# A port term in a kernel's planner, two-source work kept off GpSimd in the second half, and sums of x formed when an attention pair ends

## The chip, the core and the metric

The kernel runs on one core of a Trainium2 chip. The core has a matrix engine (TensorE, PE in the profile; PEld is its weight load, which overlaps it), three engines that work on whole tiles (VectorE or DVE, ScalarE or ACT, GpSimd or POOL) and SyncE (SP), which issues nearly all of this kernel's DMAs. The metric is the device time of one execution in microseconds. TensorE is granted one of two clocks, 1.2 or 2.4 GHz; the profile gives the granted clock of a stretch as a share of the upper one.

## What is computed

Causal attention over 4 batches of 12 heads, 448 positions and 64 columns a head; its result, laid out as 1792 rows of 768, goes through a two-layer network with a squared ReLU. Everything is float32. The reference, cut to this:

```python
scores = np.matmul(q, k.transpose(0, 1, 3, 2)) / np.sqrt(64)
scores = np.where(np.triu(np.ones((448, 448), bool), k=1), -1e9, scores)
attn = np.exp(scores - scores.max(-1, keepdims=True))
attn = attn / (attn.sum(-1, keepdims=True) + 1e-09)
x = np.matmul(attn, v).transpose(0, 2, 1, 3).reshape(1792, 768)
h = np.maximum(x @ w_in, 0.0)          # w_in 768 x 2048
return h * h @ w_out                   # w_out 2048 x 768
```

w_in and w_out arrive as 64-bit floats and are decoded on the chip.

## The kernel before

**Splits.** For the network every float32 operand is held as two fp32r tiles: a rounded copy ("hi") and the rest ("lo", the whole less hi). A product takes three matmuls: hi·hi, hi·lo, lo·hi. `split` (L297) makes both: hi by a copy on POOL or ACT, lo by a subtraction with two sources on DVE or POOL. Names: `x` (attention's result, the matmuls' moving operand), `wi` and `wo` (pieces of w_in and w_out), `g` (the squared ReLU), all with a hi and a lo; `words` is a scratch area for pieces of the weights, for x read back and for sums; `r0`..`r5` are 128x448 work tiles; `ps` is a bank of PSUM; `acc` holds the output.

**Stages.** The rows are taken in two halves (batches 0 and 1, then 2 and 3), the 2048 hidden columns in four groups. A group is an H stage (x times w_in, ReLU, square, split into g) and an O stage (g times w_out, added into acc: 14 pieces of 4 products, 168 matmuls). First the attention of head pairs 0 to 11 runs; then, during the four groups of the first half, the attention of pairs 12 to 23 is put between the matmuls. Its results wait in DRAM (`x_dram`, 12 tiles of 128x448). In the first half an H stage has 8 units of 18 matmuls (`h_unit`, L553). In the second half `h_pair` (L681) multiplies 2x2 blocks with 7 products instead of 8, by Winograd's scheme: 2 x 7 x 9 = 126 matmuls. It needs seven parts of x for each of three columns, "11", "21", "22" and the sums t1 to t4 (`x_parts`, L589: 4 loads, 4 sums, 7 splits a column, so 12 sums and 21 splits in all), and seven parts of w_in for each pair of hidden tiles (`w_parts`, L622). w_in and w_out are decoded in the first half (`piece`, L497), split, and kept in DRAM as hi and lo (`wi_split`, `wo_split`), from which the second half reads them; `w_parts` adds hi and lo again (`whole`, L632), forms sums (`made`, L667) and splits them (`done`, L662).

**What sets the order.** `Plan.emit` (L97) is a list scheduler that runs once, when the kernel is built. Each operation has a rank, dependences, tiles to take and give back, and one or more "ways": an engine and a duration from a formula (`t_dve`, `t_pool` and others, L147 to L160). It takes the ready operation that can start first, chooses the way that ends first, and so fixes the order on each engine. On the chip each engine runs its list in that order, held up by semaphores. One line gives a start: `max(free[e], at)`, the later of the engine's free time and the operands'. `attended` and `entered` (L848 on) are points in the plan behind which tiles of the attention stage and of `h_unit` may be taken for the parts of x. What stands in a tile kind at one time is bounded by caps: `r=2, xs=2, y=6` and `fz=5, s=3, xp=4`.

Of the kernel before, what the change touches and what calls it, by code (L numbers as in the profile page):

```python
# [36 lines left out]
class Plan:  # L37
# [59 lines left out]
    def emit(self):  # L97
        free = [1.0, 1.9, 3.4, 2.7, 0.7, 0.7]
        ready = [o for o in self.ops if o.left == 0]
        order = []  # L100
        while ready:
            best = None
            for o in ready:
                at = o.ready + (self.ISSUE if o.ways[0][0] >= DMA else 0.0)
                if o.take:
# [7 lines left out]
                    (max(free[e], at) + us + self.BIAS[e], max(free[e], at), i, e)  # L113
                    for i, (e, us, _) in enumerate(o.ways)
# [6 lines left out]
            free[e] = end = start + o.ways[i][1]  # L121
            order.append((start, len(order), o, i))
# [41 lines left out]
def kernel(  # L164
# [17 lines left out]
    nc = tc.nc  # L182
# [73 lines left out]
    plan.pool("r", tiles("r", NR, [P, S], F32), r=2, xs=2, y=6)  # L256
    plan.pool("f", [], fz=5, s=3, xp=4)
# [50 lines left out]
    def attention(s, n, at):  # L308
# [70 lines left out]
        def normalise(c, keys, at):  # L379
            def operands():  # L380
                return probabilities(c), probabilities(c), s.sm[:, c:c + 1]
            plan.op(at, [
                (POOL, 0.0005 * CW[c] + 0.34, lambda: nc.gpsimd.tensor_scalar(  # L383
                    *operands(), 1.0, op0=ALU.mult, op1=ALU.mult)),
                (DVE, t_dve(CW[c], True) + 0.5, lambda: nc.vector.tensor_scalar(
                    *operands(), None, op0=ALU.mult)),
# [57 lines left out]
        plan.op(at, [(DVE, 0.45, inverse)], [], keys)  # L444
# [15 lines left out]
        else:  # L460
            xs = Hold("r", "xs")
            plan.op(at, [
                on_act(S, lambda: xs.t, lambda: av.t[:, :S], True),
                (DVE, t_dve(S) + 0.05, lambda: nc.vector.tensor_copy(xs.t, av.t[:, :S])),
            ], [av], [xs], take=xs, drop=[av])
            plan.op(at, [(DMA, 0.7, lambda: nc.sync.dma_start(out=x_dram[n - NA], in_=xs.t))],
                    [xs], [("xd", n - NA)], drop=[xs])
# [4 lines left out]
    wo_dram = nc.dram_tensor("wo_split", (NG, 2 * GF, P, 2, CH), F32, kind="Internal").ap()  # L472

    def wo_part(a, ch):
        return late["wo"][:, :, a, ch * CH:(ch + 1) * CH].bitcast(F32)

    def keep(rank, kind, gr, a, ch, after):
        if kind == "i":
            def go():
                for i in range(2):  # L480
                    nc.sync.dma_start(
                        out=wi_dram[gr, :, a // CB, :, i, a % CB].rearrange("f p n -> p f n"),
                        in_=wi_t[:, i, a].bitcast(F32).rearrange("p (f n) -> p f n", n=P))
            plan.op(rank, [(DMA, 1.9, go)], [(("wi", a), 0), (("wi", a), 1)], [("wid", gr, a)], after)
            return
        plan.op(rank, [(DMA, 1.7, lambda: nc.sync.dma_start(
            out=wo_dram[gr, a + GF * ch], in_=wo_part(a, ch)))],
            [(("wo", a, ch), 0), (("wo", a, ch), 1)], [("wod", gr, a, ch)])

    def fetch(rank, gr, a, ch):  # L490
        plan.op(rank, [(DMA, 1.7, lambda: nc.sync.dma_start(
            out=wo_part(a, ch), in_=wo_dram[gr, a + GF * ch]))],
            [("wod", gr, a, ch)], [(("wo", a, ch), 0), (("wo", a, ch), 1)])
# [3 lines left out]
    def piece(rank, kind, gr, a, ch, after):  # L497
# [23 lines left out]
        def dst(i):  # L521
# [11 lines left out]
            z(), z(), 3, None, op0=ALU.logical_shift_left))], [], [zt])  # L533
        plan.op(rank - 2, [on_dve(n, z, z, b, ALU.add, 0.3)], [bt], [zt], drop=[bt])
        plan.op(rank - 2, [(DVE, t_dve(n) + 0.2, lambda: nc.vector.scalar_tensor_tensor(
            out=z(), in0=word(1), scalar=-2 ** 31, in1=z(),
            op0=ALU.bitwise_and, op1=ALU.bitwise_or))], [raw], [zt], drop=[raw])
        split(rank, n, lambda: dst(0), lambda: dst(1), zf, [zt], key, after, [zt])
        pieces.extend(plan.ops[mark:])
# [4 lines left out]
    def squared(f, h, r, rank):  # L544
        def rt():
            return r.t
        plan.op(rank, [on_dve(S, rt, rt, rt, ALU.mult, 0.4), on_pool(S, rt, rt, rt, ALU.mult),
                       on_act(S, rt, rt, func=AF.Square)], [], [r])
# [32 lines left out]
    x7, owned = {}, {}  # L581

    def combine(rank, n, dst, a, b, op, reads, writes, **kw):
        def of(h):
            return lambda: h.t[:, :n]
        plan.op(rank, [on_dve(n, of(dst), of(a), of(b), op), on_pool(n, of(dst), of(a), of(b), op)],
                reads, writes, **kw)

    def x_parts(i, rank, after):  # L589

        B = {}
        for m, (key, n) in enumerate((("11", i), ("12", NP + i), ("22", NP + CB + i), ("21", CB + i))):
# [300 lines left out]
```

## Time and profile before

| | us |
|---|---|
| time, median of 3 runs (lowest, highest) | 632.28 (631.47, 632.42) |
| the profiled execution | 631.39 |
| its span, first to last instruction | 629.6 |
| PE busy / DVE busy / ACT busy / POOL busy | 604.6 / 367.3 / 325.2 / 371.8 |
| mean granted clock of TensorE | 0.989 |

The span is what the trace covers; the profiled execution is 1.8 us longer than its span and 0.9 us shorter than the median. By the trace the attention alone lasts to about 75 us, the first half to about 401 us, the second to the end. Matmuls are pipelined: the trace shows each as 0.34 to 0.39 us long while they start about 0.2 us apart, so an unbroken stage is read from the distance of starts. A row of the waits view names who was waited for; a releaser is inferred, and where the engine named had work of its own held up, the wait began further back.

### The profile page before, as it was taken

To read this page: it belongs to the slowest core of one execution; us is meant where nothing else is said; L and a number is where in the kernel's file an instruction comes from. 1 tells how busy PE (TensorE), PEld (TensorE's weight loads), DVE (VectorE), ACT (ScalarE), POOL (GpSimd) and SP (SyncE) were. 2 spreads that over 40 slices of the span, in tenths; PEclk is the share of its full clock that TensorE was granted. 3 is DMA by queue.
4 is the path that set the end of the run, shared out by engine and by line. 5 is a ranking of instruction groups with operands and counts; after the bars stand their busy time and mean duration, and the time that the engine had idled before them with its cause. 6 is when DMAs were issued, how large, how long until landed. Compare 5 with 4: busy or idle time off the path is not lost.

```text
span 629.6 us, 11242 instructions
## 1 busy us (share of the span) xinstructions
PE 604.6 (96%) x3864; PEld 532.2 (85%) x3864; DVE 367.3 (58%) x822; ACT 325.2 (52%) x803; POOL 371.8 (59%) x454
## 2 busy tenths in 40 slices
PE   4989999999999899999999999799999999999997
PEld 2656677898888798898898889799999999999997
DVE  5679976386767788767874219944015424533222
ACT  4679896865687646587556433345235003302400
POOL 2456766644767763787846459989238706914510
PEclk9799999999999899999999999999999999999999
DMA  9877852797897899886964144873234234333022
GB/s 146 164 187 132 180 122 56 170 324 260 217 258 227 230 256 275 228 251 177 257 199 156 50 129 154 280 223 101 100 110 141 82 126 145 101 101 102 1 89 87
DMA packets 175225, 103.77 MB, mean 165 GB/s; under 512 B 115264, under 2 KB 164928, under 8 KB 175168
## 3 DMA queue, kind: packets, MB, share of 16 engines
q1 hardware_dynamic: 171456, 102.59, 58.9%
q10 hardware_dynamic: 3712, 0.46, 0.5%
q8 instruction: 30, 0.49, 0.3%
q14 instruction: 27, 0.22, 0.1%
HBM read 69.60 MB, written 33.42 MB: 164 GB/s over the span
## 4 chain that ended last, share of the span: by engine, by line
PE 60%; DVE 4%; issue 1%; DMA 1%; POOL 0%; ACT 0%; DVEq 0%; ACTq 0%
PE ps L754 9%; PE ps L756 9%; PE ps L755 9%; PE ps L693 5%; PE ps L695 5%; PE ps L697 5%; PE ps L559 3%; PE ps L561 3%; PE ps L560 3%; PE ps L417 2%; PE ps L397 2%; PE ps L357 2%; DVE x L287 1%; DVE acc L287 1%; DVE words L287 1%
## 5 line engine op out<-in xcount | busy, mean ns | idle before, releaser
L756 PE MATMUL ps<-wo,g 128*128 128x384 f32 x448 | 150.4, 336 | 2.5 <-POOL g L291 2.5
L754 PE MATMUL ps<-wo,g 128*128 128x384 f32 x448 | 152.4, 340 | 0.0
L755 PE MATMUL ps<-wo,g 128*128 128x384 f32 x448 | 150.3, 336 | 0.0
L383 POOL TENSOR_SCALAR ap<-ap,asm 128x64 f32<-128x64 f32 (+6 forms) x120 | 73.9, 636 | 43.6 <-DVE asm L442 22.2
L287 DVE TENSOR_TENSOR acc<-ps,acc 128x384 f32<-128x384 f32 x84 | 46.1, 553 | 84.1 <-PE ps L756 70.5
L284 ACT ACTIVATE r<-ps 128x448 f32<-128x448 f32 x60 | 32.8, 546 | 107.5 <-PE ps L697 79.3
L756 PEld LDWEIGHTS ps<-wo,g 128*128 128x128 f32 x448 | 84.4, 188 | 2.8 <-POOL g L291 2.8
L754 PEld LDWEIGHTS ps<-wo,g 128*128 128x128 f32 x448 | 84.5, 189 | 1.3 <-issue 0.8
L370 DVE CUSTOM_DVE_ANT_0 ps<-ps,mask 128x448 f32<-128x448 f32 (+6 forms) x168 | 68.7, 443 | 27.5 <-PE ps L357 18.3
L755 PEld LDWEIGHTS ps<-wo,g 128*128 128x128 f32 x448 | 84.6, 189 | 0.2
L284 ACT ACTIVATE words<-words 128x384 f32<-128x384 f32 (+3 forms) x112 | 64.5, 614 | 25.7 <-DMA words<-in_moe_w_in_dram 8.6
L559 PE MATMUL ps<-x,wi 128*128 128x448 f32 x192 | 74.4, 387 | 0.3 <-DVE x L287 0.3
L561 PE MATMUL ps<-x,wi 128*128 128x448 f32 x192 | 70.3, 366 | 0.9 <-POOL wi L291 0.9
L560 PE MATMUL ps<-x,wi 128*128 128x448 f32 x192 | 70.2, 365 | 0.0
L374 ACT ACTIVATE ap<-ps,mx 128x448 f32<-128x448 f32 (+6 forms) x126 | 58.7, 483 | 21.3 <-DVE mx L370 15.6
L287 DVE TENSOR_TENSOR r<-ps,r 128x448 f32<-128x448 f32 x40 | 24.9, 623 | 73.7 <-PE ps L697 71.1
L294 POOL TENSOR_SCALAR wi<-words 128x512 fp32r<-128x512 f32 (+1 forms) x27 | 15.9, 589 | 85.1 <-PE ps L695 57.2
L291 POOL TENSOR_TENSOR g<-r,g 128x448 fp32r<-128x448 f32 x50 | 59.5, 1195 | 5.5 <-ACT g L284 2.7
L284 ACT ACTIVATE r<-r 128x448 f32<-128x448 f32 x76 | 43.9, 577 | 21.8 <-DVE r L287 20.4
L693 PE MATMUL ps<-x,wi 128*128 128x448 f32 x138 | 51.3, 372 | 3.7 <-ACT r L284 3.7
L291 POOL TENSOR_TENSOR wi<-words,wi 128x512 fp32r<-128x512 f32 (+1 forms) x41 | 52.3, 1279 | 1.7
L695 PE MATMUL ps<-x,wi 128*128 128x448 f32 x138 | 51.2, 371 | 0.0
(94 smaller groups left out, 1157.4 us busy)
## 6 DMA issues: line engine op xcount, KB each, us to landing
words<-in_moe_w_in_dram SPq DMA_DIRECT2D x24, 512.0 KB, 4.8
words<-in_moe_w_out_dram SPq DMA_DIRECT2D x32, 384.0 KB, 4.1
wi_split<-wi SPq DMA_DIRECT2D x48, 256.0 KB, 3.6
wo_split<-wo SPq DMA_DIRECT2D x32, 384.0 KB, 3.9
wo<-wo_split SPq DMA_DIRECT2D x32, 384.0 KB, 5.1
wi<-wi_split SPq DMA_DIRECT2D x18, 384.0 KB, 3.5
out_dram<-acc SPq DMA_DIRECT2D x28, 192.0 KB, 1.9
v<-in_v_dram SPq DMA_DIRECT2D x24, 192.0 KB, 4.6
```

Of the source, the lines that this page charges most:

```text
L284: return (ACT, t_act(n, psum, more), lambda: nc.scalar.activation(dst(), src(), func, **kw))
L287: return (DVE, t_dve(n) + more, lambda: nc.vector.tensor_tensor(out=dst(), in0=a(), in1=b(), op=op))
L291: lambda: nc.gpsimd.tensor_tensor(out=dst(), in0=a(), in1=b(), op=op))
L383: (POOL, 0.0005 * CW[c] + 0.34, lambda: nc.gpsimd.tensor_scalar(*operands(), 1.0, op0=ALU.mult, op1=ALU.mult)),
L559: nc.tensor.matmul(o, w[:, 0], x[:, 0], start=c == 0, stop=False)
L560: nc.tensor.matmul(o, w[:, 0], x[:, 1], start=False, stop=False)
L561: nc.tensor.matmul(o, w[:, 1], x[:, 0], start=False, stop=c == NP - 1)
L693: nc.tensor.matmul(o, w.t[:, 0, c], x[:, 0], start=begin and c == 0, stop=False, skip_group_check=True)
L695: nc.tensor.matmul(o, w.t[:, 0, c], x[:, 1], start=False, stop=False, skip_group_check=True)
L754: nc.tensor.matmul(res(), g[:, 0], w[:, 0], start=f == 0, stop=False)
L755: nc.tensor.matmul(res(), g[:, 0], w[:, 1], start=False, stop=False)
L756: nc.tensor.matmul(res(), g[:, 1], w[:, 0], start=False, stop=f == GF - 1)
```

## The change

**Planner.** `emit` keeps one more time, `port`: a way marked `SHARED` starts no earlier than the last such way has ended, on whichever engine. Marked are two-source operations on DVE and POOL, and DVE's fast one-source ones; POOL's copies (L294) and its normalise operation of attention (L383) aren't. Several durations change. `two_sources` offers DVE and POOL both until `pool_too[0]` is set to False, which is done before the parts of x and the second half are planned: from there such work goes on DVE alone.

**Sums of x.** When an attention pair of the first half's stages ends, `spill` stores its result as before and, for the pairs of the last batch, also forms t1 (columns 0 to 2) or t1 to t4 from PSUM and from what it reads back, in `r` tiles, and stores those in `xt_dram`. `x_parts` is replaced by `x_part`: one load and one split for each of 21 parts, in the order of the seven products. Caps change: xs 4, xp 3, fo 2.

**Weights.** w_out is kept whole (`wo_whole`, one store of half the size), read back and split again in the second half; w_in is kept whole too for groups 1 to 3 (`wi_whole`) and split only for groups 0 and 3. So `whole` runs in group 0 alone, and parts "11", "12" and "22" of groups 1 and 2 get a split that they didn't need before. The second half runs its groups from 3 to 0, and group 3's w_out stays in SBUF. The matmuls are the same in kind and number.

```diff
@@ emit
-        order = []
+        order, port = [], 0.0
...
                 w = min(
-                    (max(free[e], at) + us + self.BIAS[e], max(free[e], at), i, e)
-                    for i, (e, us, _) in enumerate(o.ways)
+                    (max(free[w[0]], at, port if len(w) > 3 else 0.0) + w[1] + self.BIAS[w[0]],
+                     max(free[w[0]], at, port if len(w) > 3 else 0.0), i, w[0])
+                    for i, w in enumerate(o.ways)
                 )
...
             free[e] = end = start + o.ways[i][1]
+            if len(o.ways[i]) > 3:
+                port = max(port, end)
...
 def t_dve(n, fast=False):
-    return n / 1920 + 0.25 if fast else n / 960 + 0.15
+    return n / 1920 + 0.15 if fast else n / 960 + 0.15
 def t_pool(n, two=False):
-    return n * 0.0027 + 0.04 if two else n / 1200 + 0.26
+    return n * 0.0021 + 0.21 if two else n / 1200 + 0.22
...
+    def two_sources(*args):
+        return [on_dve(*args, 0.03) + SHARED] + ([on_pool(*args)] if pool_too[0] else [])
...
-        plan.op(rank, [on_dve(n, lo, src, lambda: hi().bitcast(F32), ALU.subtract, 0.4),
-                       on_pool(n, lo, src, lambda: hi().bitcast(F32), ALU.subtract)],
+        plan.op(rank, two_sources(n, lo, src, lambda: hi().bitcast(F32), ALU.subtract),
                 list(reads) + [(key, 0)], [(key, 1)], after, drop=drop)
...
-                (POOL, 0.0005 * CW[c] + 0.34, lambda: nc.gpsimd.tensor_scalar(
+                (POOL, 0.00083 * CW[c] + 0.3, lambda: nc.gpsimd.tensor_scalar(
...
+        if second and c < CB:
+            h = loaded(x_dram[c], ("xd", c))
+            less(h, [av])
+            stored(h, *t_place(1))
+        elif second:
+            t1 = loaded(*t_place(1))
+            x21 = loaded(x_dram[c], ("xd", c))
+            x12 = loaded(x_dram[n - CB], ("xd", n - CB))
+            less(t1, [av])
+            plan.op(at, two_sources(S, lambda: x21.t, lambda: x21.t, lambda: t1.t, ALU.subtract),
+                    [t1], [x21])
+            less(x12, [av])
+            stored(t1, *t_place(2))
+            stored(x12, *t_place(3))
+            stored(x21, *t_place(4))
...
+    def x_part(key, i, rank, after):
+        t, h = x7[key, i], Hold("f", "xp")
...
+        plan.op(rank - 4, [(DMA, 0.9, lambda: nc.sync.dma_start(out=h.t, in_=place))], [saved], [h], take=h)
+        split(rank, S, lambda: t()[:, 0], lambda: t()[:, 1], lambda: h.t, [h], ("x7", key, i), [after], [h])
...
-    keys = [(key, i) for key in ("11", "t2", "21", "t3", "t1", "t4", "22") for i in range(CB)]
+    keys = [(OTHER[key], i) for key in SEVEN for i in range(CB)]
+    pool_too[0] = False
...
-        for gr in range(NG):
+        for gr in range(NG - 1, -1, -1):
             begin, rank = group(ph, gr, rank, 1.0, begin)
```

Two places show what this does to the order. In the rows a line number, the operation, the tiles out<-in and the shape stand; the numbers at the names tell tiles apart.

DVE in the last O stage of the first half, before: `words<-words,r` and `r<-words,r` are sums of x or of w_in, `x2_` and `x` a lo of a part of x.

```order
L287 TENSOR_TENSOR r5_102<-words_96,r4_101 128x448
L287 TENSOR_TENSOR acc_1379<-ps6_119,acc_1379 128x384
L287 TENSOR_TENSOR x2_81<-r4_101,x2_81 128x448
L287 TENSOR_TENSOR acc_1379<-ps2_115,acc_1379 128x384
L287 TENSOR_TENSOR x0_79<-words_96,x0_79 128x448
L287 TENSOR_TENSOR x1_80<-words_96,x1_80 128x448
L287 TENSOR_TENSOR words_96<-words_96,r5_102 128x448
L287 TENSOR_TENSOR acc_1379<-ps3_116,acc_1379 128x384
```

The same place on DVE after the change:

```order
L293 TENSOR_TENSOR acc_1368<-ps4_117,acc_1368 128x384
L293 TENSOR_TENSOR acc_1368<-ps6_119,acc_1368 128x384
L293 TENSOR_TENSOR x2_3_3908<-words_96,x2_3_3908 128x448
L293 TENSOR_TENSOR x2_4_3909<-words_96,x2_4_3909 128x448
L293 TENSOR_TENSOR x2_5_3910<-words_96,x2_5_3910 128x448
L293 TENSOR_TENSOR acc_1368<-ps2_115,acc_1368 128x384
L293 TENSOR_TENSOR acc_1368<-ps7_120,acc_1368 128x384
L293 TENSOR_TENSOR x2_6_3911<-words_96,x2_6_3911 128x448
```

The sums of x are gone from this place; lo's of x in the order of the products stand between the additions into acc.

POOL where the second group of the first half goes from H to O, before: seven normalise operations of an attention pair, and behind them two lo's of g's last tile, for rows of the first and of the second batch.

```order
L291 TENSOR_TENSOR wo_1378<-words_96,wo_1378 128x384
L383 TENSOR_SCALAR ap_71<-ap_71,asm_70 128x64
L383 TENSOR_SCALAR ap_71<-ap_71,asm_70 128x128
L383 TENSOR_SCALAR ap_71<-ap_71,asm_70 128x192
L383 TENSOR_SCALAR ap_71<-ap_71,asm_70 128x256
L383 TENSOR_SCALAR ap_71<-ap_71,asm_70 128x320
L383 TENSOR_SCALAR ap_71<-ap_71,asm_70 128x384
L383 TENSOR_SCALAR ap_71<-ap_71,asm_70 128x448
L291 TENSOR_TENSOR g3_95<-r0_97,g3_95 128x448
L291 TENSOR_TENSOR g3_95<-r2_99,g3_95 128x448
```

The same place on POOL after the change, where `r1_98<-r1_98` is the square that the first of those lo's comes from:

```order
L297 TENSOR_TENSOR r1_98<-r1_98 128x448
L393 TENSOR_SCALAR ap_71<-ap_71,asm_70 128x64
L393 TENSOR_SCALAR ap_71<-ap_71,asm_70 128x128
L393 TENSOR_SCALAR ap_71<-ap_71,asm_70 128x192
L393 TENSOR_SCALAR ap_71<-ap_71,asm_70 128x256
L393 TENSOR_SCALAR ap_71<-ap_71,asm_70 128x320
L393 TENSOR_SCALAR ap_71<-ap_71,asm_70 128x384
L393 TENSOR_SCALAR ap_71<-ap_71,asm_70 128x448
L297 TENSOR_TENSOR wo_1367<-words_96,wo_1367 128x384
L297 TENSOR_TENSOR g3_95<-r4_101,g3_95 128x448
```

And DVE there after the change, with the first lo behind four operations that decode weights:

```order
L585 SCALAR_TENSOR_TENSOR words_96<-words_96 128x512
L582 TENSOR_SCALAR words_96<-words_96 128x512
L293 ISA words_96<-words_96 128x1024
L585 SCALAR_TENSOR_TENSOR words_96<-words_96 128x512
L293 TENSOR_TENSOR g3_95<-r1_98,g3_95 128x448
```

The first batch's lo of g3 has moved from POOL, behind the normalise operations, to DVE; its square has moved ahead of them.

## Rows read from the trace of the kernel before

**Rows 1.** Windows: start:end, length, busy us of each engine, granted clock, DMA share, GB/s.

```profile
0.00:48.00 48.00, 35.15 (x288) 22.35 (x290) 32.16 (x115) 31.23 (x97) 19.26 (x43) 0.93 0.85 166
48.00:75.00 27.00, 25.53 (x223) 16.44 (x219) 25.56 (x83) 24.87 (x76) 18.61 (x30) 1.00 0.88 167
205.00:217.00 12.00, 9.52 (x52) 8.96 (x51) 9.37 (x15) 8.26 (x16) 9.24 (x11) 0.87 0.84 255
217.00:371.00 154.00, 154.00 (x1032) 134.00 (x1031) 100.14 (x235) 89.94 (x224) 96.02 (x117) 1.00 0.71 198
371.00:401.00 30.00, 30.00 (x173) 29.90 (x173) 26.25 (x29) 11.09 (x22) 27.70 (x21) 1.00 0.61 199
408.00:412.00 4.00, 3.82 (x11) 3.38 (x12) 3.51 (x5) 1.59 (x5) 2.83 (x3) 0.57 0.62 196
412.00:462.00 50.00, 50.00 (x272) 48.26 (x271) 12.30 (x17) 20.43 (x40) 30.22 (x30) 1.00 0.40 126
517.00:542.00 25.00, 25.00 (x125) 22.99 (x124) 12.36 (x19) 11.03 (x20) 18.91 (x21) 1.00 0.47 147
```

**Rows 2.** Waits of PE: us in total, times, longest.

```profile
PE ps L693 <- ACT r L284: 3.7, 1, 3.7
PE ps L756 <- POOL g L291: 2.5, 1, 2.5
PE ps L561 <- POOL wi L291: 0.9, 1, 0.9
```

**Rows 3.** Timeline of PE around 404 us: start, us, line, idle before and releaser.

```profile
403.94 0.37 PE L695 MATMUL ps<-x,wi 128*128 128x448 f32 x1
404.15 0.37 PE L697 MATMUL ps<-x,wi 128*128 128x448 f32 x1
408.18 0.54 PE L693 MATMUL ps<-x,wi 128*128 128x448 f32 x1 [3.67 <-ACT r L284]
```

**Rows 4.** Timelines of ACT and DVE at the same place.

```profile
406.71 0.58 ACT L284 ACTIVATE x<-r 128x448 fp32r<-128x448 f32 x1 [2.12 <-DVE r L287]
407.61 0.52 ACT L284 ACTIVATE r<-ps 128x448 f32<-128x448 f32 x1
405.13 1.54 DVE L287 TENSOR_TENSOR r<-words,r 128x448 f32<-128x448 f32 x1
410.90 0.61 DVE L287 TENSOR_TENSOR x<-words,x 128x448 fp32r<-128x448 f32 x1
```

**Rows 5.** Groups of instructions from 371 to 408 us: count, busy us, mean ns.

```profile
L287 DVE TENSOR_TENSOR x<-words,x 128x448 fp32r<-128x448 f32 x7 | 8.8, 1273 | 0.0
L291 POOL TENSOR_TENSOR x<-words,x 128x448 fp32r<-128x448 f32 x5 | 7.3, 1463 | 0.3 <-ACT x L284 0.3
```

**Rows 6.** Timelines of POOL and DVE around 210 us.

```profile
206.03 5.49 POOL L383 TENSOR_SCALAR ap<-ap,asm 128x64 f32<-128x64 f32 x7
211.49 2.40 POOL L291 TENSOR_TENSOR g<-r,g 128x448 fp32r<-128x448 f32 x2
209.61 0.89 DVE L287 TENSOR_TENSOR wo<-words,wo 128x384 fp32r<-128x384 f32 x1
```

**Rows 7.** Groups from 516.6 to 571.6 us, one group of the second half.

```profile
L287 DVE TENSOR_TENSOR acc<-ps,acc 128x384 f32<-128x384 f32 x14 | 7.8, 558 | 19.4 <-PE ps L756 19.4
L287 DVE TENSOR_TENSOR r<-ps,r 128x448 f32<-128x448 f32 x10 | 6.2, 623 | 12.6 <-PE ps L697 12.6
L635 DVE TENSOR_TENSOR words<-wi 128x384 f32<-128x384 f32 x1 | 0.5, 547 | 0.0
L294 POOL TENSOR_SCALAR g<-r 128x448 fp32r<-128x448 f32 x6 | 3.4, 569 | 2.3 <-ACT r L284 2.3
L294 POOL TENSOR_SCALAR wi<-words 128x384 fp32r<-128x384 f32 x4 | 2.1, 514 | 19.1 <-PE ps L695 19.1
```

**Rows 8.** The page, part 6: issues of two DMAs, KB each, us from issue to landing.

```profile
x_dram<-r SPq DMA_DIRECT2D x12, 224.0 KB, 2.8
words<-x_dram SPq DMA_DIRECT2D x12, 224.0 KB, 3.3
```

More of the change, by code (lines that the diff above doesn't have):

```diff
@@ L443, in attention @@
         keys = [(nm, "sm", c) for c in range(NQ)]
-        plan.op(at, [(DVE, 0.45, inverse)], [], keys)
+        plan.op(at, [(DVE, 0.4, inverse) + SHARED], [], keys)
         for c in range(NQ):
@@ L460, in attention @@
         else:
[L461 to L467, printed above, removed]
+            spill(n - NA, av, at)
+    xt_dram = nc.dram_tensor("xt_dram", (4, CB, P, S), F32, kind="Internal").ap()
@@ new lines, with spill, result, stored @@
+    last_sums = []
+    def spill(n, av, at):
+        b, c = divmod(n, NP)
+        gate, mark = list(last_sums), len(plan.ops)
+        def result():
+            return av.t[:, :S]
+        def stored(h, place, key):
+            plan.op(at, [(DMA, 0.7, lambda: nc.sync.dma_start(out=place, in_=h.t))], [h], [key], drop=[h])
+        def loaded(place, key):
+            h = Hold("r", "xs")
+            plan.op(at - 8, [(DMA, 0.9, lambda: nc.sync.dma_start(out=h.t, in_=place))],
+                    [key], [h], gate, take=h)
+            return h
+        def less(h, drop):
+            plan.op(at, [(DVE, t_dve(S) + 0.05, lambda: nc.vector.tensor_tensor(
+                out=h.t, in0=result(), in1=h.t, op=ALU.subtract))], [av], [h], drop=drop)
+        def t_place(k):
+            return xt_dram[k - 1, c % CB], ("xt", k, c % CB)
+        second = b == 1
+        if second and c < CB:
[13 more added lines that the diff above has]
+            stored(x21, *t_place(4))
+        xs = Hold("r", "xs")
+        plan.op(at, [
+            on_act(S, lambda: xs.t, result, True),
+            (DVE, t_dve(S) + 0.05, lambda: nc.vector.tensor_copy(xs.t, result())),
+        ], [av], [xs], take=xs, drop=[av])
+        last_sums[:] = plan.ops[mark:]
+        stored(xs, x_dram[n], ("xd", n))
@@ L470 @@
     late = {"wo": None, "acc": None}
     wi_dram = nc.dram_tensor("wi_split", (NG, GF, 2, P, 2, CB, P), F32, kind="Internal").ap()
[L472 to L488, printed above, removed]
@@ L490, in fetch, with keep, go @@
-    def fetch(rank, gr, a, ch):
-        plan.op(rank, [(DMA, 1.7, lambda: nc.sync.dma_start(
-            out=wo_part(a, ch), in_=wo_dram[gr, a + GF * ch]))],
-            [("wod", gr, a, ch)], [(("wo", a, ch), 0), (("wo", a, ch), 1)])
+    wo_dram = nc.dram_tensor("wo_whole", (NG, 2 * GF, P, CH), F32, kind="Internal").ap()
+    wz_dram = nc.dram_tensor("wi_whole", (NG, GF, 2, P, CB, P), F32, kind="Internal").ap()
+    def keep(rank, gr, a, after):
+        def go():
+            for i in range(2):
+                nc.sync.dma_start(
+                    out=wi_dram[gr, :, a // CB, :, i, a % CB].rearrange("f p n -> p f n"),
+                    in_=wi_t[:, i, a].bitcast(F32).rearrange("p (f n) -> p f n", n=P))
+        plan.op(rank, [(DMA, 1.9, go)], [(("wi", a), 0), (("wi", a), 1)], [("wid", gr, a)], after)
@@ L495 @@
+    def fetch(rank, gr, a, ch):
+        h = Hold("f", "fo")
+        plan.op(rank - 6, [(DMA, 0.9, lambda: nc.sync.dma_start(
+            out=h.t[:, :CH], in_=wo_dram[gr, a + GF * ch]))], [("wod", gr, a, ch)], [h], take=h)
+        cols = slice(ch * CH, (ch + 1) * CH)
+        split(rank - 2, CH, lambda: late["wo"][:, 0, a, cols], lambda: late["wo"][:, 1, a, cols],
+              lambda: h.t[:, :CH], [h], ("wo", a, ch), drop=[h])
     pieces = []
@@ L633, in whole @@
             Z[key] = z = Hold("f", "fz")
-            plan.op(rank, [
-                (DVE, t_dve(CBW) + 0.4, lambda: nc.vector.tensor_tensor(
-                    out=z.t[:, :CBW], in0=hi(), in1=lo(), op=ALU.add)),
-                (POOL, t_pool(CBW, True), lambda: nc.gpsimd.tensor_tensor(
-                    out=z.t[:, :CBW], in0=hi(), in1=lo(), op=ALU.add))],
+            plan.op(rank, two_sources(CBW, lambda: z.t[:, :CBW], hi, lo, ALU.add),
                 reads, [z], take=z, drop=drop)
@@ L672, in w_parts @@
         done("s2")
+        direct("12")
         made("s3", "11", "21", ALU.subtract, ("11",))
@@ L768, in o_unit @@
             ways = [on_dve(CH, acc, res, acc, ALU.add)]
-        plan.op(rank, ways, [ps], [("acc", t, ch)], after if gr == 0 else (), drop=[ps])
-        if gr == NG - 1:
+        plan.op(rank, ways, [ps], [("acc", t, ch)], after if gr == first else (), drop=[ps])
+        if gr == final:
             rows = slice(ph * T + t * P, ph * T + (t + 1) * P)
```

121 lines of the change are left out of this document (61 added, 60 removed).

## The prediction, made before the changed kernel ran

> **What bounds the kernel now.** I read the windows first, stage by stage. From about 75 us on PE is the bound: it is busy for the whole of 217 to 371, 371 to 401, 412 to 462 and 517 to 542 us, at the full clock [rows 1]. The change leaves every matmul in place, so a stage with PE full can't get shorter; only what PE stands idle, or runs at the low clock, can. So the next view is the waits of PE, of which three after 75 us count: 3.7 us for ACT, 2.5 us for POOL, 0.9 us for POOL [rows 2]. Before 75 us, in the attention alone, PE stands for 12.85 us of the first 48 and 1.47 us of the next 27, where DVE (25.56) and ACT (24.87 of 27 us) are full [rows 1]. The measure for a stage is the distance of matmul starts: 30.00 / 173 = 0.173 us in an O stage, so 168 take 29.1 us; in an H stage 25.00 / 125 = 0.200 by the window and 0.21 by two starts [rows 1, 3], so I take 0.205 and 25.8 us for 126.
>
> **The largest term: the wait at 404 us.** PE starts a matmul at 404.15 and the next at 408.18, with 3.67 us idle [rows 3]. The engine named is ACT, with a copy of a PSUM bank at 407.61 that lasts 0.52 us. That copy isn't the cause. ACT stood before it for 2.12 us, for a sum on DVE (405.13, 1.54 us long), to round the sum into x at 406.71; the bank's copy was queued behind [rows 4]. DVE was late because from 371 on it and POOL both make sums and lo's with two sources, at the same time: a lo of x takes 1.27 us on DVE and 1.46 us on POOL there, while one for which POOL stood idle takes 0.61 us on DVE [rows 4, 5]. DVE is busy for 26.25 and POOL for 27.70 of the 30 us to 401 [rows 1]. And after the wait PE runs at a granted clock of 0.57 from 408 to 412: 11 matmuls take 3.82 us, not 11 x 0.205 = 2.26, which is 1.6 us more [rows 1]. The place costs 3.7 + 1.6 = 5.3 us.
>
> After the change this O stage holds no sum of x. On DVE it has about 16 lo's of x, 8 operations of 384 columns on pieces of w_in, and 14 additions into acc: 16 x 0.61 + 8 x 0.547 + 14 x 0.558 = 9.8 + 4.4 + 7.8 = 22.0 us of 29.1 [rows 4, 7]. POOL has about 15 hi's of x and a few more copies, some 22 x 0.55 = 12 us [rows 7]. If every lockable piece of the two stood one behind the other (9.8 + 4.4 + 12 = 26.2 us) it would still fit into 29.1. The parts now stand in the order of the products, so the first product waits for 3 of 21. Each part goes load, hi, lo, with three tiles for loads: (3.3 + 0.57 + 0.61 + 0.3 for hand-overs) / 3 = 1.6 us a part, or 34 us for 21 [rows 4, 7, 8], so the last is there about 4 to 5 us into the H stage and is wanted by the seventh product's x, some 11 us into it. What is late next is ACT, whose one hi of a late part still stands among its bank copies; it is ready by then at this pace. **Term: -5.3 us.**
>
> **The sums made when attention ends.** Added are 9 subtractions from PSUM on DVE, 9 x 0.62 = 5.6 us by the row of the same shape [rows 7], and 3 with both sources in SBUF, at 0.61 to 1.46 us each [rows 4, 5], and about 12 loads and 12 stores of 224 KB on SP, at 3.3 and 2.8 us [rows 8]. They spread over the last six pairs, that is mostly over 217 to 371, where PE never stands, DVE is busy for 100.14 and POOL for 96.02 of 154 us [rows 1]: that slack covers them. SP gives up more than it gains, since w_out's and w_in's stores are halved. Uncovered, DVE's part would cost 5.6 us at most. **Term: 0.**
>
> **The wait at 210 us.** In the second group's turn from H to O PE waits 2.5 us for the lo of g's last tile [rows 2]. POOL did seven normalise operations (206.03, 5.49 us) and then two lo's (211.49) [rows 6]. In the order after the change the square stands on POOL ahead of the normalise operations and the lo on DVE, behind four operations that decode weights. So the wait can vanish or be as long as those four: at the 0.5 us that DVE takes for 384 or so columns, 2.0 us. I take 0.8, nearer to nothing since DVE does them while PE still finishes the H stage. The wait was also followed by a lower clock, 0.87 over 205 to 217 [rows 1], worth at most 0.13 x 12 = 1.6 us. 2.5 + 1.6 - 0.8 = 3.3; as the clock's part is an upper end, **term: -3.2 us.** The 0.9 us wait for POOL's lo of wi [rows 2] stands behind the same operations in both orders: 0.
>
> **The attention alone.** Costs of POOL's normalise and of DVE's transposes rise or fall in the plan, and from 48 to 75 us some matmuls of the H stage come earlier in PE's list. Bounds: 0 to the 1.5 us that PE stands there. I take **-0.5 us**, since ACT, about full, doesn't get work taken away. The 12.85 us before keep PE's order, so 0.
>
> **The second half.** All lo's and sums go to DVE. At an H to O turn a lo takes DVE 0.62 in place of 1.2 us on POOL [rows 4, 6], but DVE has more queued. PE stood nowhere there before, so this can only cost: 0 to 1.5 us, **+0.4**. The pieces of w_out that must be split again (8 a group for three groups, 8 x 0.547 = 4.4 us of DVE) lie in O stages with 14 x 0.558 = 7.8 us of DVE in 29.1 [rows 7].
>
> **Sum.** -5.3 - 3.2 - 0.5 + 0.4 = -8.6 us. The profiled execution took 631.4, so 622.8; the median of the runs is 0.9 higher, so 632.3 - 8.6 = **623.7 us**. With all bounds on the good side, -5.3 - 4.0 - 1.5 = -10.8; on the bad side, -5.3 - 2.0 + 1.5 = -5.8: 621.5 to 626.5.
>
> **Rivals.** *A new wait in the first half (627.7 us).* A changed port model reorders all engines from 75 to 401 us; there are seven turns between stages where a lo could again end late. One more wait like the one at 210 us costs 2.5 + 1.6 = 4.0 us: 623.7 + 4.0. For: DVE's list at 210 us gets longer. Against: seven turns before gave one such wait.
>
> *The sums' way through DRAM (629.0).* The last pair's sums are stored (2.8 us) and loaded (3.3 us) [rows 8] before they are split, and SP issues in order, so a store that waits for its sum holds every load behind it. If the parts then come at the pace of 1.9 us or more, ACT's late hi again stands ahead of a bank copy and the 5.3 us come back: 623.7 + 5.3. Against: the first 5 of the 21 parts need nothing of the last pair.
>
> *DVE becomes the bound of the second half's H stages (634.5, slower).* There an H stage holds about 17 DVE operations with two sources in SBUF, 10 additions from PSUM and 8 lo's of g: 17 x 0.547 + 10 x 0.623 + 8 x 0.61 = 9.3 + 6.2 + 4.9 = 20.4 us [rows 4, 7]. POOL keeps 15 copies, 8 x 0.514 + 7 x 0.569 = 8.1 us [rows 7], which the planner doesn't mark as needing the port. If each holds DVE out for all its time, DVE needs 28.5 us for 25.8: 2.7 us a stage, 10.8 in four, 623.7 + 10.8. It decides against a gain once a stage loses over 2.2 us (8.6 / 4). What the trace shows of one-source work on POOL: beside the normalise operations a lo of 384 columns took DVE 0.89 us [rows 6], against 0.547 for that shape [rows 7], 0.34 more; 15 x 0.34 = 5.1 us makes 25.5, which just fits. Also against: from 517 to 542 us the engines now share 12.36 and 18.91 us of work, with PE full [rows 1]. The Trainium skill, "SBUF — State Buffer", section "Who interferes with whom", says that a VectorE instruction with two SBUF inputs contends with any GpSimd instruction that reads SBUF, and that the second to issue is fully blocked until the first ends; by that rule POOL's unmarked copies cost the full 8.1 us, while by the row they cost 5.1.
>
> *The attention alone gets faster too (618.7).* If the new order of POOL and DVE there is worth 5 of the 12.85 + 1.47 us. For: PE stands there most. Against: ACT and DVE are about full [rows 1].
>
> That the change doesn't do what it says I give nothing: the order shows no two-source operation on POOL after attention ends.
>
> **How the numbers follow.** Forecast 0.52; a new wait 0.20; DRAM 0.10; DVE the bound 0.13; faster attention 0.05. Some 0.2% (1.3 us) is about what a measurement of this kernel can tell from no change. The first two rivals in one, 633.0, or a part of the third, give no change: 0.05, taken from the first three rivals. Faster: 0.52 + 0.18 + 0.08 + 0.05 = 0.83; slower 0.12. The range reaches down to the last rival and up past the second, 618.5 to 630.0, and leaves out the slower case and some of the mixed ones.
>
> **What would show it.** Right: no wait of PE over 1 us from 400 to 415 us, a granted clock of 1.00 there, lo's of x near 0.6 to 0.9 us on DVE; a wait under 2 us at the second H to O turn; PE full from 412 us on as now. Wrong: a PE wait for x or for a bank's copy just behind the first half's end (the sums' way); waits for DVE's r, g or wi in the H stages of the second half, with DVE near 25 us busy in 25.8; or a new wait at a turn from H to O before 371 us.

## The result, and the profile after

| | before | after |
|---|---|---|
| median, us (lowest to highest, 4 runs each) | 631.88 (630.36 to 632.42) | 625.67 (624.94 to 626.97) |
| profiled execution / its span, us | 631.39 / 629.6 | 624.94 / 623.2 |
| DVE / ACT / POOL busy, us | 367.3 / 325.2 / 371.8 | 410.9 / 306.0 / 312.0 |

The ratio is 0.9908, with a 95% interval of 0.9883 to 0.9933: 5.8 us faster in ratio, 6.2 in medians, 6.4 in span. The forecast was 623.7 us. A second set of runs of the changed kernel (`after_again`, below) gave 0.9941 (0.9918 to 0.9965).

Windows of the changed kernel, columns as in [rows 1]:

```profile
205.00:217.00 12.00, 10.90 (x67) 10.40 (x66) 8.59 (x16) 8.40 (x17) 11.34 (x13) 1.00 0.76 199
217.00:371.00 154.00, 153.35 (x1027) 132.90 (x1026) 106.66 (x247) 89.94 (x225) 99.36 (x117) 1.00 0.67 189
371.00:401.00 30.00, 30.00 (x173) 29.86 (x172) 23.09 (x39) 2.00 (x5) 12.19 (x19) 1.00 0.93 312
401.00:412.00 11.00, 11.00 (x56) 10.13 (x55) 9.81 (x16) 4.17 (x8) 6.16 (x9) 1.00 0.70 220
517.00:542.00 25.00, 24.58 (x125) 22.57 (x124) 19.19 (x35) 9.14 (x16) 6.89 (x10) 1.00 0.42 134
```

PE is now full through the turn into the second half, 371 to 412 us, at the full clock; POOL's work from 371 to 401 fell from 27.70 us to 12.19. From 205 to 217 PE is busy for 10.90 us at a clock of 1.00, where it was 9.52 at 0.87 [rows 1]. But 217 to 371, full before, now has a gap, and so has 517 to 542. Rows of PE's waits that lie after 100 us (one more, 0.65 us of the transposes at 237 us, stands in a row with earlier waits):

```profile
PE ps L806 <- DVE g L293: 1.1, 1, 1.1
...
PE ps L616 <- ACT x L290: 0.6, 1, 0.6
...
PE ps L743 <- DVE r L293: 0.4, 1, 0.4
PE ps L407 <- ACT bpt L290: 0.3, 1, 0.3
PE ps L617 <- DVE x L293: 0.2, 1, 0.2
```

The 3.7 and 0.9 us of [rows 2] are gone, the 2.5 us became 1.1, and five smaller ones are new: 0.31, 0.64 and 0.19 us between 111 and 118 us, 0.65 at 237 and 0.42 at 531.7. To see what each stretch gained, I took the time that its matmuls need at the spacing of unbroken stages (0.2045 us in H, 0.1735 in O, 0.109 for a transpose, scores and products with v by their columns) from the time that it took. The level of the first three columns hangs on the price of the scores and products; the differences between kernels hardly do. The rest is PE's loss, in us; idle and low clock are both in it. "Turn" goes from the first matmul of the first half's last O stage to the first of the second half's first O stage.

| kernel | 0 to 50 us | 50 to 100 us | 100 us to turn | turn | behind it |
|---|---|---|---|---|---|
| before | 23.4 | 5.9 | 10.1 | 5.5 | 3.8 |
| after | 23.1 | 6.1 | 8.9 | -0.1 | 4.3 |
| after_again | 24.2 | 5.9 | 8.4 | -0.1 | 3.6 |
| pool_allowed | 24.2 | 5.6 | 7.5 | -0.1 | 3.5 |
| sums_at_end | 23.9 | 6.9 | 7.6 | 1.7 | 3.6 |
| sums_at_end_pool | 23.4 | 6.5 | 7.4 | 5.7 | 3.6 |
| before_dve_only | 23.0 | 6.2 | 9.9 | 8.2 | 3.8 |
| spill_only | 22.2 | 5.1 | 7.9 | -0.1 | 4.2 |
| spill_again | 23.1 | 5.5 | 9.5 | -0.1 | 4.1 |
| no_port | 24.1 | 6.7 | 17.1 | -0.1 | 4.2 |
| old_costs | 22.3 | 9.7 | 5.0 | -0.1 | 4.2 |
| copies_marked | 24.0 | 10.5 | 6.0 | 0.2 | 3.7 |
| late_port | 21.7 | 9.0 | 6.0 | 0.0 | 3.4 |
| late_port_dear | 21.3 | 8.0 | 5.5 | -0.2 | 3.3 |

Rows of the same program (after and after_again, spill_only and spill_again) differ by about 1 us in the first 50 us and by 0.5 to 1.6 between 100 us and the turn: less than that is no finding. Before to after: 5.6 us come from the turn, and nothing that can be told from elsewhere: the 1.2 from 100 us to the turn lie within that scatter, though single waits inside this stretch moved by more (below).

### The profile page after: what moved, and what is told of

It is laid out like the page before. It is cut to its first block, busy times and chain, and to the rows that moved or that the text cites. A ratio compares the mean times of both kernels' runs of the same rounds, so it can differ in the third digit from the quotient of the medians.

```text
span 623.2 us, 11325 instructions
## 1 busy us (share of the span) xinstructions
PE 601.2 (96%) x3864; PEld 528.9 (85%) x3864; DVE 410.9 (66%) x932; ACT 306.0 (49%) x768; POOL 312.0 (50%) x427
## 4 chain that ended last, share of the span: by engine, by line
PE 83%; DVE 6%; DMA 4%; ACT 3%; POOL 1%; issue 1%; SPq 0%; ACTq 0%; DVEq 0%; POOLq 0%
PE ps L804 12%; PE ps L806 12%; PE ps L805 11%; PE ps L616 6%; PE ps L427 6%; PE ps L617 6%; PE ps L618 6%; PE ps L407 5%; PE ps L743 5%; PE ps L745 5%; PE ps L747 5%; PE ps L367 4%; DVE ps L380 2%; ACT ap L384 1%; POOL ap L393 1%
## 5 line engine op out<-in xcount | busy, mean ns | idle before, releaser
L393 POOL TENSOR_SCALAR ap<-ap,asm 128x128 f32<-128x128 f32 (+6 forms) x122 | 78.2, 660 | 50.4 <-DVE asm L452 29.3
L290 ACT ACTIVATE words<-words 128x384 f32<-128x384 f32 (+3 forms) x112 | 66.7, 613 | 52.0 <-DVE words L293 10.9
L380 DVE CUSTOM_DVE_ANT_0 ps<-ps,mask 128x448 f32<-128x448 f32 (+6 forms) x168 | 68.6, 444 | 18.9 <-PE ps L367 10.1
L616 PE MATMUL ps<-x,wi 128*128 128x448 f32 x192 | 74.8, 390 | 1.2 <-ACT x L290 0.6
L305 POOL TENSOR_SCALAR wo<-words 128x384 fp32r<-128x384 f32 x44 | 27.1, 621 | 88.1 <-PE ps L806 66.0
L617 PE MATMUL ps<-x,wi 128*128 128x448 f32 x192 | 70.2, 366 | 0.2 <-DVE x L293 0.2
L618 PE MATMUL ps<-x,wi 128*128 128x448 f32 x192 | 70.1, 365 | 0.0
L305 POOL TENSOR_SCALAR g<-r 128x448 fp32r<-128x448 f32 x50 | 32.0, 642 | 53.5 <-ACT r L290 52.8
L293 DVE CUSTOM_DVE_ANT_0 words<-words 128x768 uint16<-128x768 uint16 (+1 forms) x56 | 45.4, 810 | 13.5 <-ACT words L290 10.5
L305 POOL TENSOR_SCALAR wi<-words 128x384 fp32r<-128x384 f32 (+1 forms) x43 | 28.0, 654 | 44.2 <-DVE words L585 15.4
L743 PE MATMUL ps<-x,wi 128*128 128x448 f32 x135 | 49.6, 368 | 0.4 <-DVE r L293 0.4
L745 PE MATMUL ps<-x,wi 128*128 128x448 f32 x135 | 49.5, 367 | 0.0
```

Source lines behind the costliest of these rows:

```text
L290: return (ACT, t_act(n, psum, more), lambda: nc.scalar.activation(dst(), src(), func, **kw))
L293: return (DVE, t_dve(n) + more, lambda: nc.vector.tensor_tensor(out=dst(), in0=a(), in1=b(), op=op))
L305: return (POOL, t_pool(n), lambda: nc.gpsimd.tensor_scalar(dst(), src(), 1.0, 1.0, op0=ALU.mult, op1=ALU.mult))
L380: plan.op(at, [(DVE, t_dve(w), lambda: nc.vector.tensor_tensor_reduce(out=at_(), in0=at_(), in1=mask[:, S - w:], scale=-SCALE, scalar=3.0e ...
L393: (POOL, 0.00083 * CW[c] + 0.3, lambda: nc.gpsimd.tensor_scalar(*operands(), 1.0, op0=ALU.mult, op1=ALU.mult)),
L616: nc.tensor.matmul(o, w[:, 0], x[:, 0], start=c == 0, stop=False)
```

## The experiments

**Where the sums are made, and who makes them.** Theory A: the wait of 3.7 us at 404 us went because the sums of x left this place. Theory B: because POOL no longer does two-source work beside DVE. Four kernels tell them apart.

`pool_allowed`, the changed kernel with POOL back in the second half:

```diff
-    pool_too[0] = False
```

> The changed kernel with one line taken out: POOL may do two-source work in the second half too, and by the plan does most of it. Theory A (the wait of 5.4 us at 404 us went because the sums of x are no longer made there): PE stays full at the turn into the second half, and since POOL takes the lo's of g as before, the 0.8 us wait at 531 us goes too: 625 to 626 us. Theory B (it went because POOL no longer does two-source work beside DVE): lo's of x take 1.2 to 1.5 us again on POOL, 21 of them 25 to 31 us, and at least 2 of the 5.4 us come back behind 399 us: 628 to 631 us.

Measured: 626.1 us, 0.9919 of before (0.9891 to 0.9946), turn -0.1, no wait at 531 us. Theory A's forecast. From 371 to 408 us POOL made 17 of the 19 lo's of x there, at 1.16 us each, so two-source work seldom stood on both engines at once in this run. Keeping two-source work off POOL, as such, gained nothing that these runs can tell.

`sums_at_end`, the changed kernel with `x_parts` as before, on DVE alone; the parts come column by column again (cut to the call):

```diff
...
-    for m, key in enumerate(keys):
...
-        x_part(*key, begin + (rank - begin) * (m + 0.5) / len(keys), attended if m < NX else entered)
+    for i in range(CB):
+        x_parts(i, begin + (rank - begin) * (i + 0.5) / CB, [attended, entered])
```

> The changed kernel with the old way of the sums: all 12 are made when attention is over, on DVE alone. Theory A: DVE then has 12 sums, 21 lo's of x, 8 operations on w_in and 14 additions between 370 and about 408 us; PE waits again at the turn into the second half, by 1.5 to 4 us: 627 to 630 us. Theory B: without POOL's two-source work DVE does each in 0.55 to 0.7 us, 33 x 0.62 + 8 x 0.55 + 14 x 0.556 = 33 us, of which the first products need only part: no wait over 0.5 us, 625 to 626 us.

Measured: 626.53 us, 0.9933 (0.9909 to 0.9956); the turn costs 1.7 us. The planner had put H matmuls into the O stage, and there PE waits for lo's of x while DVE has no gap. Window and PE's timeline of that kernel:

```profile
378.00:382.00 4.00, 3.17 (x15) 2.30 (x14) 4.00 (x7) 0.00 (x0) 2.36 (x4) 1.00 1.00 335
```

```profile
380.99 0.47 PE L764 MATMUL ps<-x,wi 128*128 128x448 f32 x1 [0.71 <-DVE x L293]
382.06 0.47 PE L764 MATMUL ps<-x,wi 128*128 128x448 f32 x1 [0.19 <-DVE x L293]
```

The two waits, 0.90 us, and the 1.7 us of the turn are the lower end of Theory A at most, far less than 5.5, and the time lies between the two forecasts. Theory B allowed no wait over 0.5 us.

`sums_at_end_pool`, the same with POOL allowed (the line `pool_too[0] = False` taken out too):

> The changed kernel with all 12 sums made after attention, and with POOL allowed for two-source work in the second half: against the run with the sums at the end on DVE alone, which waited 1.7 us near 379 us, this gives POOL back. Theory A: the wait at the turn is 1.5 us or more here too, for the sums are still there. Theory B (POOL beside DVE made the wait): it is larger than with DVE alone, 3 us or more. Theory D (the planner's new costs, port time included, place the same work well enough): under 1.5 us, and the time is that of the changed kernel within 1 us.

Measured: 631.52 us, 1.0008 (0.9986 to 1.0031); the turn costs 5.7 us, as much as in the kernel before. But not as Theory B has it. The windows of this kernel show DVE nearly empty and POOL full, and its groups from 368 to 405 us show POOL at the pace that it has alone:

```profile
369.00:399.00 30.00, 30.00 (x174) 29.93 (x173) 7.52 (x14) 10.17 (x20) 27.89 (x27) 1.00 0.66 214
399.00:410.00 11.00, 9.51 (x46) 8.08 (x45) 0.28 (x1) 4.22 (x9) 11.00 (x11) 1.00 0.35 108
```

```profile
L297 POOL TENSOR_TENSOR x<-words,x 128x448 fp32r<-128x448 f32 x10 | 11.4, 1154 | 0.0
L297 POOL TENSOR_TENSOR r<-words 128x448 f32<-128x448 f32 x3 | 3.5, 1159 | 0.0
```

Here nothing contends: nearly all of it went to POOL, and at 1.15 us each, 33 operations and more don't fit. The kernel's text shows why. The port time makes both ways of an operation begin at the same moment, and `emit` adds a fixed price to a way's end, `BIAS`, 1.0 us for DVE and nothing for POOL. So the way that ends first doesn't always win: the plan prefers POOL's 1.15 us to DVE's 0.65 + 1.0. No run changed `BIAS`. The wait comes from too much work on too slow an engine.

`before_dve_only`, the kernel before with DVE alone for two-source work from the parts of x on (one of four places):

```diff
...
-        plan.op(rank, [on_dve(n, of(dst), of(a), of(b), op), on_pool(n, of(dst), of(a), of(b), op)],
+        plan.op(rank, [on_dve(n, of(dst), of(a), of(b), op), on_pool(n, of(dst), of(a), of(b), op)][:2 if pool_too[0] else 1],
...
```

> The kernel before with one edit: from the parts of x on, two-source work goes on DVE alone; its planner, its sums and its weights stay. Theory A: the sums still stand between attention's end and the first product, so at least half of the wait at 404 us stays (2.5 us or more): 629 to 632 us. Theory B: the wait shrinks to under 1 us, and the time falls by 4 to 5.4 us: 626.5 to 628 us. The first half up to 371 us should stay as it is, with the waits at 170 and 210 us.

Measured: 633.42 us, 1.003 (1.001 to 1.0051), the turn 8.2 us; the time lies above both forecasts. Its planner also drew H matmuls into the O stage, and they wait three times:

```profile
381.08 0.47 PE L697 MATMUL ps<-x,wi 128*128 128x448 f32 x1 [1.30 <-DVE x L287]
384.00 0.47 PE L695 MATMUL ps<-x,wi 128*128 128x448 f32 x1 [2.25 <-POOL x L296]
385.90 0.74 PE L697 MATMUL ps<-x,wi 128*128 128x448 f32 x1 [1.43 <-DVE x L287]
```

So PE's order moved as well, and this run isn't a clean test of B; it only shows that B's edit alone doesn't bring the gain.

**The sums alone.** `spill_only` is the kernel before with `spill`, `x_part` and their caps (xs 4, xp 3), and nothing else of the change (cut to the two calls):

```diff
...
+            spill(n - NA, av, at)
...
+        x_part(*key, begin + (rank - begin) * (m + 0.5) / len(keys), attended if m < NX else entered)
```

> The kernel before with one part of the change: t1 to t4 are formed when an attention pair ends and stored, and the parts of x are only loaded and split, in the order of the products. The planner's costs, the split weights, the order of the groups and POOL's two-source work stay as before. Theory A (the place of the sums decides): the turn into the second half has no wait, the waits at 170 and 210 us stay: 5.4 us less than before, 625 to 627 us. Theory C (it takes the planner's port time as well, since DVE and POOL still hold each other up): 2 us or more are left of the wait at the turn, 628 us or more.

Measured: 623.52 us, 0.9885 (0.9855 to 0.9916); the turn costs nothing. Theory A's turn, and a time below its range. Of the two waits that were to stay, the one at 170 us did (0.93 us); the one at 210 us is gone without any of the planner's change, and one like it came a group later, behind seven normalise operations on POOL again:

```profile
297.95 0.44 PE L781 MATMUL ps<-wo,g 128*128 128x384 f32 x1 [2.08 <-POOL g L291]
```

And DVE and POOL hold each other up there as much as before. Groups from 367 to 404 us:

```profile
L287 DVE TENSOR_TENSOR x<-words,x 128x448 fp32r<-128x448 f32 x7 | 8.2, 1182 | 0.0
L291 POOL TENSOR_TENSOR x<-words,x 128x448 fp32r<-128x448 f32 x12 | 16.1, 1360 | 0.0
```

A lo of x takes 1.18 and 1.36 us, near the 1.27 and 1.46 of [rows 5], and PE stands for nothing. The contention was there, and isn't what PE waited for once the 12 sums were gone. Theory C falls. What this run doesn't part is the place of the sums from the order of the parts: `x_part` also brings the parts in the order of the products, where `x_parts` went column by column, and no run keeps the sums at the end in that order. The same kernel again, beside the changed one:

> The sums of x alone, planner and all else as before, a second time. If the sums are the whole gain, it is as fast as the changed kernel or faster by up to 3 us, that is 0.985 to 0.991 of the kernel before. If its lead over the changed kernel (623.5 to 625.7 us) was chance, the two agree within 0.2%.

> The changed kernel itself, beside the two runs below on one chip: 0.990 to 0.992 of the kernel before, with its waits near 116, 206, 236 and 531 us. If those waits come from the order of the plan they stand again at the same matmuls; if they are chance of one execution they move.

Measured on one chip: the sums alone 624.13 us, 0.9894 (0.9864 to 0.9923); the changed kernel 625.97 us, 0.9941 (0.9918 to 0.9965). The intervals touch, so the sums alone are at least as fast as far as these runs can tell, and the rest of the change together shows no gain. The changed kernel's ratio lies above the 0.990 to 0.992 that was expected. Its waits stand at the same matmuls again near 118, 212 and 237 us (0.64, 0.87 and 0.44 us idle); the one at 531 us is absent, so that one is not fixed by the order.

**What the port time does to the plan.** `no_port` never raises it:

```diff
-                port = max(port, end)
+                port = 0.0
```

> The changed kernel with the port time never raised in the planner: all other costs, sums and weights stay. Theory P (the port time is what changed the first half): the 3.1 us that went at 210 us and the 1.2 us at 170 us come back, the new waits near 116 and 236 us (1.7 and 1.0 us) go, the turn into the second half stays without a wait: 626 to 628 us. Rival Q (the new durations and the tile caps did it, not the port time): the waits stand where they stand now, within 0.5 us, 625 to 626 us.

Measured: 634.77 us, 1.0071 (1.0045 to 1.0098): worse than expected. Between 100 us and the turn PE loses 17.1 us. Theory P has the direction and not the places, Q neither: no wait came back at 170 or 210 us. The largest one behind 100 us stands at the next group's turn from H to O, behind normalise operations on POOL again:

```profile
308.93 0.57 PE L806 MATMUL ps<-wo,g 128*128 128x384 f32 x1 [2.94 <-POOL g L297]
```

With all of the change but the port time the plan loses 7.0 us more there than the kernel before; the port time makes up for that and 1.2 us more. `old_costs` keeps the port time and restores the durations (cut):

```diff
...
-    return n * 0.0021 + 0.21 if two else n / 1200 + 0.22
+    return n * 0.0027 + 0.04 if two else n / 1200 + 0.26
...
-                (POOL, 0.00083 * CW[c] + 0.3, lambda: nc.gpsimd.tensor_scalar(
+                (POOL, 0.0005 * CW[c] + 0.34, lambda: nc.gpsimd.tensor_scalar(
```

> The changed kernel with the port time kept but the durations of POOL's two-source work, copies and normalise operations and of DVE's fast operations as before. Without the port time and with the new durations the first half lost 9.7 us against the changed kernel. If the port time alone makes up for that, this run lies within 1.5 us of the changed kernel, 624 to 627 us, with no wait over 1.5 us at 210 us. If port time and durations only work as a pair, the first half loses again, 629 us or more.

Measured: 625.23 us, 0.991 (0.9881 to 0.9939). The time is as expected, but the parts move: 5.0 us from 100 us to the turn, with no wait over 0.4, and 9.7 between 50 and 100, 3.8 more than before; 3.7 us of it is one wait, at 64.8 us, for a copy on ACT. `copies_marked` extends the port time to POOL's copies and normalise operations (cut to the two places):

```diff
...
-            dst(), src(), 1.0, 1.0, op0=ALU.mult, op1=ALU.mult))
+            dst(), src(), 1.0, 1.0, op0=ALU.mult, op1=ALU.mult)) + SHARED
...
-                    *operands(), 1.0, op0=ALU.mult, op1=ALU.mult)),
+                    *operands(), 1.0, op0=ALU.mult, op1=ALU.mult)) + SHARED,
```

> The changed kernel with the planner's port time extended to POOL's copies and normalise operations, by the view that these hold DVE's two-source work off as well. If the plan gets nearer to the chip by that: the new waits at 116, 206 and 236 us (1.7, 1.4 and 1.0 us) and the 0.8 us at 531 us shrink, 622 to 625 us. If the view is too strict (a copy holds DVE off for 0.1 to 0.3 us of its 0.5 to 0.6): work is spread too far and PE waits more in the first half, 627 us or more.

Measured: 625.85 us, 0.9921 (0.9891 to 0.9952). The waits behind 100 us shrink (6.0 us), the attention alone loses 10.5: neither expectation, and no gain.

**A version that beats both.** `late_port` has the old durations, the port time only for operations that the plan starts after 80 us, and POOL allowed in the second half (cut to the port time):

```diff
...
-            if len(o.ways[i]) > 3:
+            if len(o.ways[i]) > 3 and start > 80.0:
```

> The changed kernel with the old durations, with the port time raised only by operations that the plan starts after 80 us, and with POOL allowed in the second half. With the old durations and the port time from the start, the attention alone lost about 4 us on PE between 50 and 100 us, and the first half after 100 us had no wait over 0.4 us. If the port time costs only where ACT and DVE are full, that loss goes and the rest stays: 618 to 621 us, faster than both kernels. If not, PE waits 3 us or more between 50 and 100 us again, and the time is 622 us or more.

Measured: 620.5 us, 0.9845 (0.9817 to 0.9873), on the chip where the changed kernel gave 0.9941: faster than the kernel before and than the changed one. Against the sums alone on that chip (0.9894) it is likely faster, but the intervals overlap. Which of its three differences from the changed kernel made the gain isn't shown. The reason given for it was only half right, since 50 to 100 us still lose 9.0. `late_port_dear` adds the price of 0.4 us on DVE's two-source work (cut to that price):

```diff
...
-        return [on_dve(*args, 0.03) + SHARED] + ([on_pool(*args)] if pool_too[0] else [])
+        return [on_dve(*args, 0.4) + SHARED] + ([on_pool(*args)] if pool_too[0] else [])
```

> The run with the port time after 80 us and the old durations still lost 9.2 us of PE time between 50 and 100 us, where the kernel before lost 6.0, so the port time wasn't what cost there. This run puts back the last price that favoured DVE: a two-source operation on DVE is dearer by 0.4 us in the plan, as before, and not by 0.03. If that price is what loaded DVE in the attention alone, the loss between 50 and 100 us falls to 6 or 7 us and the time to 617 to 619 us. If it is something else, the loss stays over 8 us and the time near 620.5 us.

Measured, on a third chip: 621.94 us, 0.9892 (0.9877 to 0.9908); its profile has the shortest span of all profiles, 618.9 us, and 8.0 us lost between 50 and 100. The price explains at most 1 of the 3 us, inside the scatter. What costs in the attention alone under these plans is open, as is which of the two is faster.

## Why the prediction was right, and where its sizes were off

*The wait at 404 us (-5.3).* Measured -5.6: right in size. Its cause was named as two things at once, sums in this place and DVE and POOL holding each other up. The runs part them: with the sums gone it is zero whether POOL works there or not, contending or not; with the sums still there it is 1.7 us on DVE and 5.7 on POOL in the new plan, and 8.2 on DVE in the old one. So the sums in this place made the wait, as the late sum that ACT stood for there shows too [rows 4]. How much of it goes with the engine (0.61 us an operation against 1.15), with the plan's order of matmuls or with the order of the parts, the runs leave open. The pace of the parts was right: the 21 lo's of x begin 1.6 us apart, and none was waited for, though DVE took 0.73 us for one and not 0.61. (No row shows the 0.3 us for hand-overs in that pace.) The margin was partly luck. The first lo began only at 377.01 us, 7 us into the O stage, so the last ended at 409.04, 9.8 us into the H stage and not 4 to 5, some 1.2 us before PE began the last product at 410.22. The group's row of the changed kernel:

```profile
L293 DVE TENSOR_TENSOR x<-words,x 128x448 fp32r<-128x448 f32 x20 | 13.8, 727 | 0.2 <-POOL x L305 0.2
```

*The sums when attention ends (0).* Right: with the sums alone, PE lost no more between 100 us and the turn (7.9 and 9.5 us) than before (10.1).

*The wait at 210 us (-3.2).* Locally right: the loss fell from 4.5 to 1.4 us. The way was as forecast. On DVE the lo stands behind decode operations, and PE waits for it, 1.10 us and not 0.8. The four operations took 2.7 us (0.71, 0.41, 0.69 and 0.91) and not 2.0: they are 512 and 1024 columns wide, and 0.5 us was read from 384. Timelines of the changed kernel:

```profile
210.08 0.91 DVE L585 SCALAR_TENSOR_TENSOR words<-words 128x512 int32<-128x512 int32 x1
210.91 0.61 DVE L293 TENSOR_TENSOR g<-r,g 128x448 fp32r<-128x448 f32 x1
```

```profile
211.57 0.44 PE L806 MATMUL ps<-wo,g 128*128 128x384 f32 x1 [1.10 <-DVE g L293]
```

But the stretch from 100 us to the turn gained only 1.2 us (1.7 in the second execution), where the forecast had 3.2. And `spill_only` lost the wait at 210 us with the planner as before, so that wait can go without the port time. The step that was mis-sized is the first rival's, "a new wait in the first half", held to be a case apart with one price of 4.0 us. It came in small: 1.7 us between 110 and 117 us, where PE needs x of the last pair while DVE does one of the normalise operations, and 0.9 at 236 us, where transposes wait for POOL. And the wait at 170 us, put down as staying, went with its 1.3 us. New small waits should have stood in the sum as a cost of this reordering, about 2 us. Timelines of DVE, ACT and PE of the changed kernel at the two new places:

```profile
115.73 0.45 DVE L395 TENSOR_SCALAR ap<-ap,asm 128x448 f32<-128x448 f32 x1
116.13 0.54 ACT L290 ACTIVATE x<-ps 128x448 fp32r<-128x448 f32 x1 [0.87 <-PE ps L427]
116.73 0.47 PE L616 MATMUL ps<-x,wi 128*128 128x448 f32 x1 [0.64 <-ACT x L290]
236.96 1.20 PE L407 MATMUL ps<-ident,ap 128*128 128x128 f32 x9 [0.65 <-POOL ap L393]
```

*The attention alone (-0.5).* -0.1 up to 100 us (-0.3 and +0.2): nothing.

*The second half (+0.4).* +0.5 in the first execution, -0.2 in the second: nothing that these runs can tell.

*DVE as the bound of the second half (634.5 us).* It didn't come. From 517 to 542 us DVE is busy for 19.19 us of 25, and PE for 24.58. POOL's copies do cost: the mean lo of w_out, made beside them, is 0.774 us and that of parts in `w`, nearly without, 0.548. The 0.23 us between them is a mean of two kinds: 17 of the 24 lo's began beside a running copy and took 0.85 to 0.89 us, the other 7 took 0.54 to 0.55. So a meeting costs 0.31 to 0.34, the price taken from [rows 6], but not every operation meets a copy. Groups of the changed kernel from 425 us on, and a timeline of DVE and POOL with one lo beside a copy and one without:

```profile
L293 DVE TENSOR_TENSOR wo<-words,wo 128x384 fp32r<-128x384 f32 x24 | 17.6, 774 | 20.2 <-POOL wo L305 20.2
L293 DVE TENSOR_TENSOR w<-words,w 128x384 fp32r<-128x384 f32 x7 | 3.8, 548 | 0.0
L305 POOL TENSOR_SCALAR wo<-words 128x384 fp32r<-128x384 f32 x24 | 15.4, 650 | 66.1 <-PE ps L806 66.0
```

```profile
511.48 0.86 DVE L293 TENSOR_TENSOR wo<-words,wo 128x384 fp32r<-128x384 f32 x1
512.26 0.55 DVE L293 TENSOR_TENSOR wi<-words,wi 128x384 fp32r<-128x384 f32 x1
511.43 0.51 POOL L305 TENSOR_SCALAR wi<-words 128x384 fp32r<-128x384 f32 x1
```

The Trainium skill, "SBUF — State Buffer", section "Who interferes with whom", has the two contend for one port pair that one of them holds alone. The rows agree that copies and two-source work hold each other up (POOL's copy is 0.65 us in the mean here and 0.514 in [rows 7]). And they show what the later one loses: the lo at 511.48 ended 0.40 us after the copy that it met, so it lost 0.31 of the 0.46 us that the copy still had to run, and not a copy's whole length.

*The sums' way through DRAM (629.0).* It didn't come: in every kernel that forms the sums in `spill` the turn costs 0.2 us or less.

Worked out again with the measured sizes: -5.6 at the turn, -1.2 from 100 us to it, -0.1 before, +0.5 behind, -6.4 us, which is the difference of the spans. Of the 2.2 us that the forecast of -8.6 had too much, 2.0 lie between 100 us and the turn.

## What to carry to other kernels

Take work out of the stage in which the bounding engine waits for it before making that work cheaper there: the 12 sums, formed earlier where DVE and POOL had slack, and parts then brought in the order of the products, gave the whole gain, and the rest of the change together added nothing that the runs can tell. When a change lets a planner draw a new order, put a cost for new small waits into the sum, and test each part alone, because the parts aren't additive: here the change without the port time lost 8 us more between 100 us and the turn than with it, and with the old durations it lost 4 us less there than with the new ones, and as much more before it.

## What the runs showed of the hardware

The clock: before, PE stood for 2.48 us near 210 us, and the window 205 to 217 shows a granted clock of 0.87. After, it stood for 1.10 us at the same place, and the same window shows 1.00. In `spill_only` PE stood for 2.08 us at 298 us, and the window 292 to 304 shows 1.00 too. Not all of a wait's price scales with its length: shortening this one took away all that the low clock cost.

```profile
292.00:304.00 12.00, 9.92 (x68) 8.55 (x66) 7.84 (x15) 6.24 (x11) 8.71 (x10) 1.00 0.95 254
```

A program's own time moves more than its waits: the same list of instructions lost 23.1 and 24.2 us in the first 50 us, and the changed kernel's 12 runs on one chip lay between 624.16 and 630.3 us, so a difference under 2 us between two kernels' times says little. The stretches of a trace show where such a difference lies, but they move as well, by up to 1.6 us in the same program.
